# Block-sparse attention fused with a gated FFN: PSUM as eight banks that are taken singly or in pairs, with a new order of all work

## The chip, the cores and the metric

The kernel runs on one core of one Trainium2 chip. The time is that of the device, in microseconds (us): the median over several executions of the same program. Beside it there is one profiled execution, taken by the hardware profiler, whose records give the start and end of every instruction on each engine. The engines are PE (TensorE, matrix multiplications; PEld is its loading of weights), ACT (ScalarE), DVE (VectorE), POOL (GpSimd) and SP (SyncE); POOL and SP do nothing here but issue transfers. An "L352" is line 352 of the kernel.

## The reference: what is computed

Attention for 4 batches, 8 heads, 768 positions and a head dimension of 64, with a mask of 32 x 32 blocks, and behind it an FFN on the 3072 tokens, 512 to 1536 to 512, with a sigmoid gate. Cut to what matters:

```python
scores = scale * np.matmul(q, k.transpose(0, 1, 3, 2))          # scale = 1/8
mask = np.abs(blk_i - blk_j) <= 1                               # blocks of 32
mask = mask | (blk_i == 0) | (blk_j == 0) | (blk_i == n_blocks - 1) | (blk_j == n_blocks - 1)
...                                                             # and 3 sampled key blocks a query block
scores = np.where(mask, scores, -1000000000.0)
attn = softmax(scores)                                          # written out in the reference
x = np.matmul(attn, v)                                          # heads side by side: [3072, 512]
gate = 1.0 / (1.0 + np.exp(-(x @ w_gate)))
out = gate * (x @ w_val) @ w_out
```

## The kernel before: units, tiles and an order written out by hand

**Units.** The work is cut into 12 units: 4 batches times 3 blocks of 256 queries (`UQ`). A unit has four head pairs (`Pair`, L599), a pair has three steps of 256 keys (`Step`, L554). One step is one *score job*: eight matmuls of 64 rows (`qk`, L562) write the scores of two heads into two banks of PSUM, an exp on ACT (L586, 1024 columns) brings them as P to SBUF, and a product with the mask on DVE (L592) clears what is masked. Unit 0 has no product: there, eight more matmuls (from `bias` and `mb`, the mask as rows, and `e`, a constant that spreads them) add the mask to the scores ahead of the exp.

When the three steps of a pair are through, P times V follows (PV). In units 0 and 1 (`WIDE_PV`) it has 24 matmuls of 128 rows (`pv`, L611), a reciprocal (L655) and a product (L656), together called the norm, and four transposes on PE with a copy (`turn`, `evac`), which give xT, the FFN's input. In later units PV is done in 64-row halves (`pv_parts`, L626), a reduction on DVE folds the two halves (L646), and the turn is a transposing DMA on SP's queue (`xbar`, L705).

**FFN.** It goes by groups of units (`GROUPS`: units 0 to 3 alone, then in twos). `Ffn.f` (L774) multiplies xT by the weights of gate and value (wg, wv), ACT makes a tanh of half the gate half (L801; the sigmoid is written as tanh), DVE makes (tanh + 1) times the value half (L804). `y` (L858) multiplies by wo; ACT or DVE copies the rows out with a factor 0.5 (L886, L888) and SP stores them (L878). The very last rows go through `y_last` (L944). Unit 0's FFN (`WIDE`) is in matmuls of 128 rows, all others' in 64-row halves that take turns on two banks (`turns`, L354). In unit 0 the first two jobs (`EARLY`) are cut in two: the first three quarters need three of the four head pairs.

**PSUM.** Four tiles of two banks (128 x 2 x 512 float32), `units_ps[0]` to `[3]`, named m0 to m3 (m in the profile). Each job takes a whole pair of banks, a small one too: a mask tile (two matmuls of 256 columns and a copy, `mask_tiles`, L436), a transposition of q or k (`halves`, L460; `prep`, L478), a 128-row PV, a turn. Nearly all matmuls are issued in one line (`tiled`, L352).

**Loads.** All of q, k, v and the weights come through POOL's DMA queue (L226, L236, L241). Batch 0 and the weights come in a fixed sequence (`FIRST`); for batches 1 to 3 each of 36 loads of two heads is a task of its own, which waits for the last copy that reads the old contents, and for a score job that the order names. For batch 0, q and k are transposed on PE; from batch 1 on, DVE pairs the heads up (L525) and SP's queue transposes (L536). DVE copies v beside a column of ones (`vcopy`, L545).

**The order.** `Plan` (L122) holds some 1200 tasks. `ORDER` is a list of tokens that says in which order they are issued, hence the sequence on every engine and queue:

```python
i, eng, slot, gate = re.fullmatch(r"(\d+)([PADGS]?)(?::(\d))?(?:@(\d+))?", token).groups()
```

`34:1` is task 34 with its result in PSUM pair 1; `8D` is task 8 on DVE (`A`: ACT); `105@30` is load 105, which waits for score job 30; `j3` issues idle matmuls into pair 3 (`idle`, L325), which keep PE running while it has nothing else. The costs that stand at each `plan.add` are for the program that found the order; they don't enter the kernel.

Of the kernel before, what the change touches and what calls it, by code (L numbers as in the profile page):

```python
# [16 lines left out]
ALU = mybir.AluOpType  # L17
# [14 lines left out]
PE, ACT, DVE, DMA, SP = "PADGS"  # L32
# [4 lines left out]
EARLY = 2  # L37
# [3 lines left out]
j3 j3 j3 j3 j3 j3 j3 j3 5A 8D j3 0 11A j3s 9:0 j3s j3s j3s 10D j3s j3s 12:1 1:2 j3s 13A 3:0 2 j3s 34:1 4D 35 15:2  # L41
j3s 32:3 16D 6:0 33 17:1 7D 117:2 18D 97:0 118D 44:1 98A j3s 22:3 78:2 23D 45 36:0 79D 20:3 37 21D
40:2 25:1 30:3 41 26D 76:0 77D 46:1 31 54:2 19 74:0 47 75D 27:3 24 55 50:0 28D 80:1 64:3 51 81D
48:2 65 60:1 49 56:0 61 14 66:3 58:2 67D 105@30 57 29 89:3 59 38:1 90 52:0 86:2 53D 87 39 68:3
93:0 69D 62:1 108:2 94 42:3 109 43D 102:0 63D 111:3 70:1 103 110 126:2 71D 112 104 95:0 84:1 96D
122:3 85A 113 140:0 127 123 91 130:1 128 132:3 141 129 131 72:2 119:0 99:1 73D 133 120 147:2 134
100 135 142 157:0 148 154:3 171:1 124 155 149 158 88 164:3 143:2 156 176:0 92@164 144 121 146@111
101 172 170@44 165 173 161:2 217@54 145 190:1 177 189@46 162 125@40 178 237@54 159 186:3 191 150:2
115:0 151D 192 174:2 187 116 204:1 175 188 231:0 179:3 183:2 232 205 180D 244:3 184 233 206 166
245 82:0 200:2 218 83D 201 246 234:3 193:0 219 194A 152 235 185 153 211:2 136:0 220 137D 212 138  # L50
272:3 195 139 229 223A 202 167:0 255:2 168 236 273 213 221A 239 214:0 230 307:1 274 169 215 275
256 240 216 197:3 308 257 196 181 198 258 248:0 309 182 199 241:2 249 242 310 268:3 262 225:1 250
260 114@268 263 269 251 252:2 226 318:0 261 207:3 319 253 315:1 208 289:2 316 160@315 254 106:0
265:3 243 290 107A 247@265 266 270 276:1 209 291 300:0 293:3 277 301 278 282:1 294 292 283 297 163
303:0 335:2 295 302 222 304 279 227 285:1 336 296 286 238 359:0 305 337 360 210 284 331:3 228
362:1 348 332 361 264 349 363 333 328:0 287 350 329 267 322:3 351A 320 344:1 353A 311:0 323
203@344 345 341:2 387:3 321@359 312 342 317 271@282 426:1 373:0 313 411@300 427 330 397:2 374 398
343 388 346 375 259 408:1 376 389 355:2 400@268 409 390 347@30 419:0 356 334@89 380:3 405:1 428
370:2 381 306@111 364 420 288@44 406 371 386@214 366:3 421 410 365@265 454:2 422 433:1 455 432@380
# [3 lines left out]
442 474:1 484:0 463A 378 465A 339 467:2 452 340 475 524:3 480 485 525 514 354 515:1 327 468 486  # L63
# [4 lines left out]
538 583 438 550:1 567 571 542 439 586 551 638:0 563:2 572 425 539 564 552 595:1 573A 404 577:2 604  # L68
639 574 596 578 609:0 568 597 555 575A 627:2 598 616:3 610 628 617 543@616 635:1 565 712@200 630:2
611 569@300 636 612 592:3 446@563 688:0 631 593 658@60 689 654 706:1 556@231 588:3 707 579 641@550  # L70
640 642:0 632 676@471 619:1 633 589 587@282 620 594 691@214 623:2 690 613 590 670:1 591 643 671
637 605:3 624 644 621 606 645 659:1 618 625 709:0 681:3 710 626 660 607 655:2 682 692:0 656 453
663:3 711 726@99 661 657 608@234 673:2 693 662 674 622@652 664 672 694 548 699:1 695 665 723:2 666
# [3 lines left out]
762 669 782 730:3 745A 734:0 760 757:2 731 735 753 798:3 703 758 799 732 736 764:0 759 750 743A  # L77
600 765 797 826:3 823:1 767 763 824 650 816:0 766 651 827 809:1 756 768 810 719 800 787:3 817 769
733 788 806:1 801:0 807 770D 819:3 789 772A 811 737:1 790:2 839 738 614 802 580 615 791 803 601
# [5 lines left out]
904 856 925 936:0 978:1 913 937 911 857 919:3 979 908 875:0 920 914 876 929:1 921 917A 905 932  # L85
970:3 930 935 971 877 922 946:0 915A 1024:3 931 947 893 1025 928 1027:2 1012:0 939 938 916 1013
948 959:3 1028 966 1040:0 940 960 1041 1026 941 967:2 973:3 944A 942D 968 945 1029 952:0 1001:1
# [6 lines left out]
1078 1074 1094 1008 1082 1095 1083 1084 1100:1 1087A 1096A 1108:3 1088 1098A 1101 1085A 1099 1097  # L94
# [3 lines left out]
1163:2 1154D 1164 1159 1156D 1155 1157 1165 1160 1166 1167 1168:0 1161 1169 1170 1162 1171 1172  # L98
"""
GAP, PV_HALF, PV_PARTS, F_HALF, Y_ONE = 0.3, 0.36, 0.74, 0.875, 0.216  # L100
# [14 lines left out]
class Bank:  # L115


    def __init__(self):
        self.slot = None


class Plan:  # L122
# [14 lines left out]
    def run(self):  # L137
        done = set()
        for token in self.order:
            if token[0] == "j":  # L140
                self.idle(int(token[1]), token[2:])
                continue
            i, eng, slot, gate = re.fullmatch(r"(\d+)([PADGS]?)(?::(\d))?(?:@(\d+))?", token).groups()
            i = int(i)
            engines, fn, deps, more = self.tasks[i]
            assert i not in done and done.issuperset(deps)
            done.add(i)
            if slot is not None:
                more["take"].slot = int(slot)
# [7 lines left out]
def kernel(  # L157
# [159 lines left out]
    units_ps = [ps.tile([128, 2, 512], f32, name=f"m{i}") for i in range(4)]  # L317

    def both(bank):
        return units_ps[bank.slot]  # L320

    def both16(bank):
        return units_ps[bank.slot].bitcast(f16)

    def idle(unit, kind):  # L325
        n = 1 if kind == "s" else 4
        for i in range(2):
            rows = slice(i * D, (i + 1) * D)
            nc.tensor.matmul(
                units_ps[unit][:, i, 0 : n * 128].rearrange("a (x n) -> a x n", n=128),  # L330
# [61 lines left out]
    rings["pr"] = [qp[:, p] for p in range(NP)]  # L392
# [42 lines left out]

    def mask_tiles(c0, c1, j):  # L436

        bank = Bank()

        def mm(eng):  # L440
            for i in range(2):
# [716 lines left out]
```

## Time and profile before

| | before |
|---|---|
| median of 3 runs | 277.87 us (277.65, 277.87, 278.82) |
| the profiled execution: span | 277.8 us |
| its last instruction ends (end of the chain of waits) | 277.84 us |
| granted TensorE clock in it | 0.999 |
| first matmul that isn't idle work | 4.64 us |
| first FFN matmul | 23.94 us |
| last matmul ends | 274.69 us |
| instructions on PE, DVE, ACT, POOL | 5007, 421, 243, 69 |
| moved by DMA | 28.93 MB |

How to read it: the span runs from the first to the last record of the profiled execution; its difference to the median (0.03 us) is smaller than the spread of the runs. "Busy" is the share of the span in which an engine had an instruction at work; as matmuls are pipelined and their ends are modelled, a busy PE is not PE at its peak, and the pace of PE is better read from one matmul's start to the next one's. A matmul of 256 columns starts every 0.11 us; two 64-row matmuls that lie in different halves of the array run beside each other and share this time. In the page's second part the span is cut into 40 slices of 6.9 us with the busy tenths of each: PE has 8, 8, 7, 9 in the first four, then 9 throughout and 5 in the last.

### The profile page before, as it was taken

What the parts mean: (1) busy time and instruction counts of PE and PEld (TensorE: products, weight loads), DVE (VectorE), ACT (ScalarE), POOL (GpSimd) and SP (SyncE); (2) the same over time, 40 slices, a digit from 0 to 9 for tenths busy, and PEclk for the clock granted to TensorE, in tenths of its full rate; (3) what the DMA queues carried; (4) which work ended last, traced back from release to release, by engine and by line L of the source; (5) the groups of instructions that cost most, each with busy time, mean ns of one, the idle gap of its engine ahead of it and who ended that gap; (6) DMA issues with size and microseconds to landing.
All of it is one profiled execution on the core that took longest, in us unless ns stands there. A gap on an engine that the chain in (4) does not pass through costs nothing.

```text
span 277.8 us, 11169 instructions
## 1 busy us (share of the span) xinstructions
PE 270.0 (97%) x5007; PEld 178.7 (64%) x5007; DVE 207.1 (75%) x421; ACT 192.1 (69%) x243; POOL 47.3 (17%) x69
## 2 busy tenths in 40 slices
PE   8879999999999999999999999999999999999995
PEld 3667785896897798655566655655655676555543
DVE  4667788899999989978988886887876899004422
ACT  3988868899989958968868965679688571035300
POOL 7776261030480000028300000000000000000000
PEclk9999999999999999999999999999999999999999
DMA  7999999994599693339986743014130002230004
GB/s 160 175 195 197 200 205 198 140 139 100 84 160 145 117 140 97 103 98 167 142 113 113 73 61 97 2 21 142 24 96 4 4 2 76 70 151 2 0 2 151
DMA packets 56684, 28.93 MB, mean 104 GB/s; under 512 B 33036, under 2 KB 53692, under 8 KB 56636
## 3 DMA queue, kind: packets, MB, share of 16 engines
q0 software_dynamic: 21520, 13.90, 35.7%
q1 hardware_dynamic: 34628, 14.02, 24.8%
q8 instruction: 39, 0.64, 1.0%
q10 hardware_dynamic: 488, 0.30, 0.3%
q14 instruction: 9, 0.07, 0.1%
HBM read 28.47 MB, written 6.29 MB: 125 GB/s over the span
## 4 chain that ended last, share of the span: by engine, by line
PE 87%; DMA 7%; POOL 2%; ACT 1%; DVE 1%; issue 1%; SPq 0%
PE m L352 86%; DMA q<-in_q_dram 3%; DMA v<-in_v_dram 2%; DMA kT<-kp 1%; ACT P L586 1%; POOL k L226 1%; POOL q L226 1%; POOL wg L236 0%; POOL wv L236 0%; DVE ysb L888 0%; DVE P L592 0%; ACT ysb L886 0%; PE m L472 0%; PE m L467 0%; ACT ysb L929 0%
## 5 line engine op out<-in xcount | busy, mean ns | idle before, releaser
L586 ACT ACTIVATE P<-m 128x1024 f16<-128x1024 f32 x144 | 143.1, 1025 | 27.8 <-PE m L352 24.6
L352 PE MATMUL m<-xT,wg 64*128 64x512 f16 (+2 forms) x720 | 136.7, 326 | 0.1
L352 PE MATMUL m<-xT,wv 64*128 64x512 f16 (+2 forms) x720 | 136.7, 326 | 0.0
L592 DVE TENSOR_TENSOR P<-P,mask 128x1024 f16<-128x1024 f16 x132 | 87.0, 684 | 2.7 <-ACT P L586 2.6
L352 PEld LDWEIGHTS <-wg 64*128 64x128 f16 (+1 forms) x720 | 66.6, 94 | 21.2 <-issue 0.8
L352 PEld LDWEIGHTS <-wv 64*128 64x128 f16 (+1 forms) x720 | 66.4, 94 | 18.2 <-issue 0.5
L804 DVE SCALAR_TENSOR_TENSOR ht<-th,m 128x512 f16<-128x512 f32 x72 | 49.0, 685 | 37.0 <-ACT th L801 36.1
L352 PE MATMUL m<-wo,ht 64*128 64x512 f16 (+2 forms) x564 | 70.4, 372 | 0.0
L801 ACT ACTIVATE th<-m 128x512 f32<-128x512 f32 x72 | 42.8, 598 | 29.6 <-PE m L352 26.1
L352 PE MATMUL m<-qT,kT 64*128 64x256 f16 x576 | 53.6, 269 | 0.9 <-DMA kT<-kp 0.5
L352 PEld LDWEIGHTS <-P 64*128 64x128 f16 (+1 forms) x2112 | 41.1, 94 | 5.2 <-issue 0.4
L352 PEld LDWEIGHTS <-ht 64*128 64x128 f16 (+1 forms) x564 | 29.4, 94 | 23.4 <-issue 1.3
L352 PE MATMUL m<-vex,P 64*128 64x65 f16 (+1 forms) x2112 | 42.5, 190 | 0.0
L352 PEld LDWEIGHTS <-kT 64*128 64x128 f16 x576 | 26.7, 94 | 17.8 <-issue 1.3
L646 DVE TENSOR_REDUCE acc<-m 128x260 f32<-128x520 f32 x40 | 27.8, 697 | 7.9 <-PE m L352 6.8
L226 POOL DMA_DIRECT2D k<-in_k_dram x15 | 11.1, 744 | 48.3 <-PE m L352 45.0
L886 ACT ACTIVATE ysb<-m 128x512 f32<-128x512 f32 x18 | 10.2, 601 | 11.8 <-PE m L352 11.8
L656 DVE TENSOR_TENSOR x<-acc,rz 128x256 f16<-128x256 f32 x40 | 17.0, 425 | 1.4
L226 POOL DMA_DIRECT2D v<-in_v_dram x16 | 11.6, 736 | 33.5 <-PE m L352 12.9
L226 POOL DMA_DIRECT2D q<-in_q_dram x19 | 13.9, 733 | 3.9 <-DMA wo<-in_moe_w_out_dram 1.8
L352 PE MATMUL m<-bias,e 64*128 64x256 f16 x48 | 5.9, 271 | 2.3 <-DVE mask L299 1.9
L929 ACT ACTIVATE ysb<-m 128x256 f32<-128x256 f32 x1 | 0.4, 383 | 10.1 <-PE m L352 10.1
(47 smaller groups left out, 84.1 us busy)
## 6 DMA issues: line engine op xcount, KB each, us to landing
out_dram<-ysb SPq DMA_DIRECT2D x23, 256.0 KB, 2.4
v<-in_v_dram POOLq DMA_DIRECT2D x16, 192.0 KB, 5.1
k<-in_k_dram POOLq DMA_DIRECT2D x15, 192.0 KB, 6.6
q<-in_q_dram POOLq DMA_DIRECT2D x12, 192.0 KB, 6.4
wg<-in_moe_w_gate_dram POOLq DMA_DIRECT2D x6, 256.0 KB, 8.4
wv<-in_moe_w_val_dram POOLq DMA_DIRECT2D x6, 256.0 KB, 9.0
wo<-in_moe_w_out_dram POOLq DMA_DIRECT2D x3, 512.0 KB, 12.8
xT<-x SPq DMA_TRANSPOSE x40, 2.4
```

What stands on the lines that cost most here:

```text
L226: return nc.gpsimd.dma_start(dst[:, h0:h1, t0:t1, :], src[b, h0:h1].rearrange("h (p t) d -> p h t d", t=NT)[:, :, t0:t1, :],)
L352: return nc.tensor.matmul(out, lhsT, rhs, start=start, stop=stop, skip_group_check=True).ins
L586: nc.scalar.activation(self.pt.rearrange("a h i n -> a (h i n)"), both(self.bank).rearrange("a h n -> a (h n)"), AF.Exp, bias=0.0, scale=SCALE
L592: nc.vector.tensor_tensor(self.pt, self.pt, m.unsqueeze(1).broadcast_to([128, 2, 2, UQ]), op=ALU.mult,)
L646: nc.vector.tensor_reduce(self.acc.rearrange("a h s d -> a (h s d)"), self.parts.rearrange("a r n -> a n r"), axis=mybir.AxisListType.X, o ...
L656: nc.vector.tensor_tensor(self.x16.rearrange("a s h d -> a h s d"), self.acc[:, :, :, 0:D], rz.broadcast_to([128, 2, 2, D]), op=ALU.mult,)
L801: nc.scalar.activation(th, both(bank)[:, 0, :], AF.Tanh, bias=0.0, scale=0.5)
L804: nc.vector.scalar_tensor_tensor(self.ht[:, tiles[0] : tiles[-1] + 1, :], in0=th.rearrange("a (f n) -> a f n", n=self.w), scalar=1.0, in1= ...
L886: nc.scalar.activation(ysb, both(bank)[:, s, :], AF.Copy, bias=0.0, scale=0.5)
L929: nc.scalar.activation(ysb, src, AF.Copy, bias=0.0, scale=0.5)
```

## The change

**PSUM.** One tile of eight banks, `m` [128, 8, 512]. `units_ps[0]` to `[3]` are now views of two banks each, and `one(bank)`, `one16(bank)` give a single bank, named by the letters a to h (a and b are the halves of pair 0). A slot in `ORDER` may be a digit (a pair) or a letter (one bank), and the letter Q is a new "engine" that picks a task's single-bank form for the planner.

```diff
-    units_ps = [ps.tile([128, 2, 512], f32, name=f"m{i}") for i in range(4)]
+    banks = ps.tile([128, 8, 512], f32, name="m")
+    units_ps = [banks[:, 2 * i : 2 * i + 2, :] for i in range(4)]
...
+    def one(bank):
+        i = "abcdefgh".index(bank.slot)
+        return units_ps[i // 2][:, i % 2, :]
```

**Small work in one bank.** The two mask rows up to 512 columns, the mask tiles, the transpositions of q, k and x (`halves` becomes `turned_in` and `turned_out`) and the PV of units 0 and 1 may take one bank. A mask tile in one bank has both its matmuls in rows 0 to 63, one after the other, where in two banks they lie in different rows; a transposition in one bank is one of 128 x 128 in place of two or four of 64 rows.

```diff
-                    both(bank)[:, i, 0 : c1 - c0],
-                    e64[i * D : (i + 1) * D, t * 128 : (t + 1) * 128],
-                    mb24[i * D : (i + 1) * D, c0:c1],
-                    True,
-                    True,
+                    half(i), e64[rows, t * 128 : (t + 1) * 128], mb24[rows, c0:c1], True, True
...
+        def half(i):
+            return one(bank)[:, i * w : (i + 1) * w] if bank.single else both(bank)[:, i, 0:w]
...
+                rows = slice(0, D) if bank.single else slice(i * D, (i + 1) * D)
```

**FFN of units 0 and 1 in pieces.** For groups below `SMALL = 2`, `Ffn.f` gives way to `f1`, which makes one feature tile: eight matmuls of 128 rows and 256 columns into one bank, a tanh of 256 columns and a product of 256 columns, where `f` makes two feature tiles in two banks with 512 columns each. So unit 1, which was in 64-row halves, is now in 128 rows as well. `EARLY` goes from 2 jobs to 4 pieces. The ring of tanh results is halved for them (`th1`).

```diff
-EARLY = 2
+EARLY, SMALL = 4, 2
...
+        def f1(self, f):
...
+                def mm(eng):
+                    for c in cs:
+                        for g in range(2):
+                            bank.last = tiled(
+                                one(bank)[:, g * UQ : (g + 1) * UQ],
+                                (wg, wv)[g][:, c, f * 128 : (f + 1) * 128],
+                                self.x[:, c, :],
+                                c == 0 and g == 0,
+                                c == 3 and g == 1,
+                            )
...
+            def tanh(eng):
+                nc.scalar.activation(th, one(bank)[:, 0:UQ], AF.Tanh, bias=0.0, scale=0.5)
...
+            if self.g == 0 and f < EARLY:
+                a = plan.add(
+                    [(PE, 0.659)],
+                    go(range(3)),
...
+                a = plan.add([(PE, 0.22)], go(range(3, 4)), [a] + xdone[0][3:], mode="W")
```

**The last rows.** `y_last` writes to one bank instead of the first of two.

**The planner's view.** All costs at `plan.add` are new, and tasks carry what they need of the first transfers (`needs`), their mode on PE and the queue of their transfer; transfers of loads, stores and transposes are planned as one queue (`dma="L"`, `"O"`, `"T"`, `"X"`). None of it enters the kernel but by the order.

**The order.** `ORDER` is all new. The first lines of it, before and after:

```diff
-j3 j3 j3 j3 j3 j3 j3 j3 5A 8D j3 0 11A j3s 9:0 j3s j3s j3s 10D j3s j3s 12:1 1:2 j3s 13A 3:0 2 j3s 34:1 4D 35 15:2
-j3s 32:3 16D 6:0 33 17:1 7D 117:2 18D 97:0 118D 44:1 98A j3s 22:3 78:2 23D 45 36:0 79D 20:3 37 21D
+8 11A 5 j2 j2 j2 j2 j2 j2 j2 j2 j2 6Q:a 9:1 12:2 0 1:b 3:3 13 2 10 7A 30:0 15:1 4A 31 16 34:3 35
+17Q:e 18 117Q:f 118 97Q:c 98 44:0 45 82Q:d 83 20:2 21 32:3 33 80Q:c 81 36:0 37 22Q:d 23 74Q:e
```

What the two programs hold, counted from their instructions: 5007 matmuls before and 4861 after (128-row ones take the place of 64-row pairs, idle ones go from 19 tokens to 9); 235 activations on ACT before and 245 after; 79 and 93 gate and bias products on DVE; copies on ACT 7 and 5, on DVE 67 and 69. POOL's 65 and SP's 64 transposing and 27 copying transfers are the same, and each of the 36 later loads has its gate in both. The first FFN matmul is the 438th matmul before and the 378th after. From it to the end, PE changes 15 times between 128-row and 64-row work before, and 32 times after.

More of the change, by code (lines that the diff above doesn't have):

```diff
@@ L31 @@
 NU = S // UQ
-PE, ACT, DVE, DMA, SP = "PADGS"
+PE, ACT, DVE, DMA, SP, ONE = "PADGSQ"
 VB = 5
@@ L46 @@
[L46 to L57, printed above, removed]
@@ L429 @@
         ),
-        [(DVE, 0.42)],
+        [(DVE, 0.335)],
     )
     t_rows = [
-        rows(S, lambda eng, spread: copy(eng, mb24, spread), [(DVE, 0.95), (ACT, 0.82)])
+        rows(S, lambda eng, spread: copy(eng, mb24, spread), [(DVE, 0.87), (ACT, 0.70)])
     ]
@@ L498, in turn @@
                 tiles = [pr[:, t, :] for t in range(t0, t1)]
-            halves(both16(bank), tiles)
+            turned_in(bank, tiles)
         def evac(eng):
@@ L664, in turn @@
             x16 = self.x16.rearrange("a s h d -> a s (h d)")
-            halves(both16(self.bank2), [x16[:, s, :] for s in range(2)])
+            turned_in(self.bank2, [x16[:, s, :] for s in range(2)])
         def evac(self, eng):
@@ L692, in value @@
                 a, free = plan.add(
[L693 removed]
+                    [(DVE, 0.609)], self.fold, [a] + folded[-3:-2], free=self.bank
                 ), None
             self.normed = plan.add(
[L696 removed]
+                [(DVE, 0.55)], self.norm, [a] + before("x16", self.i), free=free
             )
@@ L748, in scores @@
             take=run[0][1].bank,
-            ops=16 if first else 8,
+            score=True,
+            needs=("e0", "e1") if first else (),
         )
@@ L753, in scores @@
             e = plan.add(
-                [(ACT, 0.98)], st.exp, [a] + before("P", 3 * pr.i + st.j), free=st.bank
+                [(ACT, 0.903)], st.exp, [a] + before("P", 3 * pr.i + st.j), free=st.bank
             )
@@ L844, in f @@
                     take=bank,
-                    lag=GAP,
-                    ops=16 * self.per,
+                    needs=wneeds,
                 )
                 a = plan.add(
-                    [(PE, F_HALF)], half(False), [a], ops=16 * self.per
+                    [(PE, 0.863 if self.w == 512 else 0.872)], half(False), [a], turn=True
                 )
             used["xT"][self.g].append(a)
-            c = plan.add([(ACT, 0.57)], tanh, [a] + before("th", i), free=bank, part=1)
-            g = plan.add([(DVE, 0.68)], gate, [c], free=bank, part=1)
+            old = before("th", i)
+            if i < len(rings["th"]) and used["th1"]:
+                old = [x for m in (2 * i, 2 * i + 1) for x in used["th1"][max(k for k in used["th1"] if k % 6 == m)]]
+            c = plan.add([(ACT, 0.477)], tanh, [a] + old, free=bank)
+            g = plan.add([(DVE, 0.598)], gate, [c], free=bank)
             used["th"][i] = [g]
@@ L898, in part @@
                     take=bank if first and f0 == 0 else None,
-                    lag=0.0 if f0 < 8 else GAP if first else None,
-                    ops=16,
+                    turn=not first and f0 == 0,
+                    needs=(f"o{f0 // 4}",),
                 )
```

296 lines of the change are left out of this document (176 added, 120 removed), and 50 rows, old and new, of the table ORDER.

## The prediction

> **What bounds the kernel now.** I read the page's busy line first, then the chain of waits, then busy time in five stretches.
>
> ```profile
> span 277.8 us, 11169 instructions
> ...
> PE 270.0 (97%) x5007; PEld 178.7 (64%) x5007; DVE 207.1 (75%) x421; ACT 192.1 (69%) x243; POOL 47.3 (17%) x69
> ```
> ```profile
> 206.30 68.39 PE m L352 x884
> ...
> 274.71 0.38 ACT ysb L929
> ```
> ```profile
> 0.00:24.00 24.00, 19.99 (x438) 13.71 (x439) 14.70 (x41) 17.80 (x21) 17.75 (x28) 1.00 1.21 180
> 24.00:60.00 36.00, 35.94 (x668) 28.50 (x666) 29.74 (x62) 29.72 (x39) 10.85 (x16) 1.00 1.24 179
> 60.00:160.00 100.00, 99.47 (x2172) 70.33 (x2170) 90.23 (x186) 84.57 (x104) 18.66 (x26) 1.00 0.76 119
> 160.00:240.00 80.00, 79.88 (x1447) 47.96 (x1441) 61.98 (x120) 50.48 (x65) 0.00 (x0) 1.00 0.20 51
> 240.00:277.80 37.80, 34.67 (x307) 18.21 (x302) 10.47 (x16) 9.50 (x17) 0.00 (x0) 0.99 0.16 58
> ```
>
> The columns are the stretch, its length, then the busy time of PE, PEld, DVE, ACT and POOL, the granted clock, the DMA share and GB/s. From 24 us on PE is busy 250.0 of 253.8 us, and 3.1 us of the rest lie behind its last matmul (274.69). So the kernel has two parts: a start of 24 us in which PE waits for others, and 250 us in which its own stream is the bound. A gain must come from the start, from the few holes later, or from a shorter stream. The start in rows of the timeline (start, duration, engine, line, what; in brackets the idle time and what ended it):
>
> ```profile
> 5.67 0.27 PE L413 MATMUL m<-e,mb 64*128 64x256 f16 x1
> ...
> 15.36 0.29 PE L352 MATMUL m<-bias,e 64*128 64x256 f16 x2 [1.91 <-DVE mask L299]
> 15.47 0.29 PE L352 MATMUL m<-qT,kT 64*128 64x256 f16 x2
> ...
> 19.70 0.91 PE L352 MATMUL m<-vex,P 128*128 128x65 f16 x24
> 20.54 0.23 PE L467 MATMUL m<-const,x 64*128 64x64 f16 x4
> ...
> 22.85 0.61 PE L352 MATMUL m<-qT,kT 64*128 64x256 f16 x8 [0.29 <-DVE x L656]
> 23.69 0.32 PE L472 MATMUL m<-const,q 64*64 64x64 f16 x16 [0.23 <-DMA q<-in_q_dram]
> 23.94 0.28 PE L352 MATMUL m<-xT,wg 128*128 128x256 f16 x1
> ```
> ```profile
> 6.73 1.94 ACT L586 ACTIVATE P<-m 128x1024 f16<-128x1024 f32 x2 [0.86 <-PE m L352]
> 8.56 0.59 ACT L297 CAST mask<-m 128x512 f16<-128x512 f32 x1
> 9.17 5.69 ACT L586 ACTIVATE P<-m 128x1024 f16<-128x1024 f32 x6
> 16.01 4.82 ACT L586 ACTIVATE P<-m 128x1024 f16<-128x1024 f32 x5 [1.15 <-PE m L352]
> ```
> ```profile
> 14.35 0.36 DVE L545 COPY vex<-v 128x768 f16<-128x768 f16 x1 [1.53 <-DMA v<-in_v_dram]
> 14.63 0.68 DVE L299 CAST mask<-m 128x512 f16<-128x512 f32 x1
> ...
> 17.49 0.18 DVE L655 RECIPROCAL rz<-m 128x4 f32<-128x4 f32 x1 [0.60 <-PE m L352]
> 17.70 0.42 DVE L656 TENSOR_TENSOR x<-m,rz 128x256 f16<-128x256 f32 x1
> ```
>
> PE's real supply opens with the first FFN matmul (23.94): it needs unit 0's outputs, so all twelve exps of unit 0, which ACT makes one after another. In them lie a mask copy (0.59) and a hole of 1.15 us: PE stood 1.91 us for a PSUM pair that DVE had not emptied, because a v copy at the head of DVE's queue waited 1.53 us for its load and a mask copy stood behind it.
>
> **The change part by part.** The sum is made on the profiled execution: span 277.84, the same as its chain's end; the median of the runs is 277.87, so 0.03 is added at the end.
>
> *One tile of eight banks.* The names change, no instruction. In the built program each wait of PE for ACT or DVE still goes with a bank or operand that both touch, so I count nothing.
>
> *The start.* First exp: it needs the bias row and ACT free. ACT now also copies the 768-column mask row before it; ACT's 383 and 601 ns for 256 and 512 columns (rows below) extrapolate to 0.82. Its second matmul ends at 5.94 (5.67 above), so it ends near 6.75, and the first exp stays at 6.7 to 6.8. Then twelve exps: two took 1.94 and six 5.69, so each further one 0.94 and one alone 1.0. The mask copies are all on DVE now and go through single banks, so the next scores have pairs of their own. The v copies are ordered behind the masks, not in front. By the order, scores 11 and 12 stand behind two PVs, each with a norm of 0.6; I allow 0.5 for that. Its end: 6.7 + 11 x 0.94 + 1.0 + 0.5 = 18.5. Now the twelfth is the fourth of the five at 16.01: 16.01 + 3 x 0.94 + 1.0 = 19.8. After it stand: the turn and copy of pair 1 (0.2 + 0.3) behind which DVE's norm of pair 2 waits (0.6), PE's PV of pair 3 and two scores beside it, then turn, copy, and FFN: 0.2 + 0.3 + 0.2, with semaphores and a mode change 0.6 more: 2.7 us. FFN opens at 21.2. In the kernel before that stretch takes 4.1 us, with the q transposes ahead of FFN waiting for their load (0.23); they now come after three FFN pieces. Bounds for this term: 20.6 (no wait of scores 11 and 12) to 22.5 (DVE one mask copy and one norm later).
>
> The work that PE has left then: in the order of instructions 437 matmuls stand ahead of the first FFN matmul before, 377 after. Left over additionally are one score job and one q turn (0.22 + 0.11); three mask tiles and one turn are done (0.33 + 0.05). Net -0.05. The mask tiles cost PE twice as much in one bank (their halves run one after the other, 9 x 0.11 = 1.0), but all nine lie before FFN, where PE has room.
>
> *Does FFN find its weights?*
>
> ```profile
> 20.66 0.75 POOL L236 DMA_DIRECT2D wv<-in_moe_w_val_dram  x1
> ```
> ```profile
> wv<-in_moe_w_val_dram POOLq DMA_DIRECT2D x6, 256.0 KB, 9.0
> ```
>
> The fourth pair of weight blocks (feature tiles 6 and 7) is issued last at 20.66 and lands 9.0 later, at 29.7. In the new order it is used behind six FFN pieces (eight matmuls 0.11 apart, by 25.05 and 25.16 below, 0.88 each), nine score jobs of 0.22, one PV of 0.73 (19.70 to 20.54, less one change of mode), turns of 0.3 and twelve mode changes of 0.1: 21.2 + 9.5 = 30.7. Margin 1.0, so nothing; the other blocks have as much.
>
> *Mode changes.* The new order alternates 128-row work (FFN of units 0 and 1) with 64-row work (scores, PV parts). Rows of the same timeline at such a place:
>
> ```profile
> 25.05 0.27 PE L352 MATMUL m<-xT,wg 128*128 128x256 f16 x1
> 25.16 0.27 PE L352 MATMUL m<-xT,wv 128*128 128x256 f16 x1
> 25.36 0.23 PE L467 MATMUL m<-const,x 64*128 64x64 f16 x4
> 25.43 0.27 PE L352 MATMUL m<-mb,e 64*128 64x256 f16 x2
> 25.54 0.84 PE L352 MATMUL m<-qT,kT 64*128 64x256 f16 x8
> ```
>
> 0.20 from the last 128-row start to the next, where 0.11 is the pace: a change costs 0.09 to 0.10. From the first FFN matmul to the end the order has 15 such changes before and 32 after: 17 x 0.10 = +1.7. Bounds: 0 (the wait falls in a hole anyway) and 1.7. I take 1.7, since PE has no holes there. The Trainium skill, page "TensorEngine Tiling (Array Packing)", section "Tiling Modes", says the same against the change: changing the tiling mode, not just the tile, drains the engine. It gives no price there; by the 128 cycles at 2.4 GHz that the Trainium skill's page "TensorE: Matmul & The Clock Gate", section "Part 2: What happens when you issue a matmul", gives for a drain, an estimate is 0.053 a change, 0.9 in all, and the sum would be 0.8 lower. The trace agrees that a change stalls, and at 0.09 it measures the higher price.
>
> *Unit 1 in 128 rows, and half-size pieces.* A pair of 64-row matmuls of 256 columns also goes every 0.11 (15.36, 15.47). So the 96 matmuls of unit 1 cost the same to what two decimals tell, 0 to 0.3; taken 0.1. ACT and DVE do 24 tanhs and gates of 256 columns in place of 12 of 512:
>
> ```profile
> L886 ACT ACTIVATE ysb<-m 128x512 f32<-128x512 f32 x18 | 10.2, 601 | 11.8 <-PE m L352 11.8
> ```
> ```profile
> L929 ACT ACTIVATE ysb<-m 128x256 f32<-128x256 f32 x1 | 0.4, 383 | 10.1 <-PE m L352 10.1
> ```
>
> 24 x 0.383 - 12 x 0.601 = +2.0 us of ACT, and by DVE's 0.42 (L656, 256 columns) and 0.68 (L299, 512) 1.9 there, within 20 to 65 us, where each is busy 0.83 of the time (24 to 60): hidden. Without that cover it would cost at most 2.0.
>
> *Holes in the dense part.* Three are to be seen:
>
> ```profile
> 121.35 0.90 PE L352 MATMUL m<-vex,P 64*128 64x65 f16 x48
> 122.78 0.39 PE L352 MATMUL m<-qT,kT 64*128 64x256 f16 x4 [0.53 <-DMA kT<-kp]
> ```
> ```profile
> 205.80 0.38 PE L352 MATMUL m<-qT,kT 64*128 64x256 f16 x4
> 206.30 0.37 PE L352 MATMUL m<-xT,wg 64*128 64x512 f16 x1
> ```
>
> 0.53 for batch 2's transposes; 0.28 at 206 (0.50 passes where four score matmuls at 0.11 a pair need 0.22); 0.23 at 25.54 (eight score matmuls took 0.84, 0.61 at 22.85). Sum 1.0, removed. For the first: in the order the loads of batch 2 stand 12 to 19 us of PE work earlier (one 48), those of batch 3 38 to 57, on the same gpsimd queue, and the two transposes that the late scores read stand 18 and 22 us ahead of their use. New holes of the new order: from below 0; from above one of 0.5 in each of the three stages, 1.5. I take 0.5. The DMAs are the same in number and bytes.
>
> *The end.* y of the last unit in single banks: same matmuls, the last ACT copy (0.38) and store stay: 277.84 - 274.69 = 3.15. Half a MB more of output leaves within the last 8 us, issued before the last three copies, so 0 (to 0.5).
>
> Sum: 21.2 + (274.69 - 23.94 = 250.75) - 0.05 + 1.7 + 0.1 - 1.0 + 0.5 = 273.2 for PE's last matmul; + 3.15 + 0.03 = **276.4**.
>
> **The rivals.** A measurement of this kernel tells about 0.5% (1.4 us) from no change, so "faster" is below 276.5, "slower" above 279.3.
>
> *B, the start keeps its length.* DVE has three more copies of 0.68 in the stage where it already stood behind loads; if a norm or v copy waits behind two of them, FFN opens at 22.5 and the mode changes eat the rest: 277.7. For it: the chain from 16 to 24 us runs over DVE. Against it: DVE was busy only 14.7 of the first 24 us.
>
> *C, slower: pieces wait for their bank.* In unit 1's FFN banks a and b are used four and three times, with about 2.05 us of PE work between a piece's end and the next one in its bank (one piece 0.88, one PV 0.73, two scores 0.22 each). The bank is free after a tanh (0.38) and a gate (0.43); if an exp (1.02) and a mask product (0.68) stand ahead of them, after 2.5. Each of the 24 pieces of units 0 and 1 that finds that waits 0.45; PE runs in order, so all later work waits too. It decides the sign from seven pieces on (3.1 us: 279.5); eight give 280.0. For: ACT and DVE are at 0.83 there. Against: the order puts the tanh before the queued exps at most places, and eight banks serve.
>
> *D, all goes well.* The changes of mode fall where PE would wait for a bank, and no hole comes: 276.4 - 1.7 - 0.5 = 274.2. Against it: the rows show the 0.09 between streams that waited for nothing.
>
> That nothing is gained because the banks still depend on each other as one tile is the case that the change does not do what it says; it would serialize PE with ACT at each score job (144 x 1 us), and the built program's waits exclude it; no chance is kept.
>
> **How the numbers follow.** Forecast A 0.55, with its own range 275.4 to 277.3 (0.36 of it under 276.5, 0.19 within the bound); B 0.18 (0.17 the same, 0.01 slower); C 0.13 (slower); D 0.14 (faster). Faster 0.50, same 0.36, slower 0.14. The range leaves out C's 0.12 and the lower half of D, 0.07: 274.6 to 278.8. Its ends are also what the open terms give: start 20.6, no changes' price in part and no holes; start 22.5 with 1.5 us of holes.
>
> **What would show it.** The first FFN matmul at 21.2 +- 0.6; the last exp of unit 0 at 18.5; no idle row of 1 us between 7 and 21 us on ACT; 0.2 from start to start at each change from 128 to 64 rows, 32 of them after; no wait for kT near 122; PE busy all but 1 us from 24 us to its last matmul near 273.2; 3.1 us behind it. Wrong it would be by waits of PE for tanh or gate of units 0 and 1 (C), by a first FFN matmul later than 22 (B), or by a hole in the middle whose releaser is a DMA: a load that a DVE copy waits for with products queued behind it.

## The result, and the profile after

The change makes the kernel slower: 297.52 us (median of 4 runs, 295.99 to 298.0) against 278.35 us (median of 4), a ratio of 1.065 with a 95% interval of 1.060 to 1.070. The forecast was 276.4. Ratios and intervals, here and below, leave out executions in a slow state, so a ratio can differ a little from that of the medians.

The page of the kernel after, in its parts 1, 2 and 4 (PEclk is the granted clock and DMA the busy share of the DMA engines, in tenths, one digit for 7.4 us):

```profile
span 296.1 us, 10891 instructions
...
PE 277.1 (94%) x4861; PEld 187.6 (63%) x4861; DVE 210.2 (71%) x437; ACT 190.3 (64%) x251; POOL 47.2 (16%) x69
...
PEclk9999999799979989999999999999999999999999
DMA  8999998979999996983300201221011101001013
...
PE 78%; DVE 8%; DMA 8%; issue 3%; SPq 1%; ACT 1%; DVEq 0%
```

The same stretches as before (length, busy time of PE, PEld, DVE, ACT, POOL, then the granted clock, the DMA share and GB/s):

```profile
0.00:24.00 24.00, 22.22 (x401) 15.45 (x402) 17.58 (x49) 19.09 (x22) 18.51 (x29) 1.00 1.21 177
24.00:60.00 36.00, 32.17 (x573) 23.49 (x572) 28.32 (x65) 27.30 (x42) 9.47 (x14) 0.95 1.16 176
60.00:160.00 100.00, 89.81 (x1910) 71.69 (x1904) 85.62 (x181) 77.51 (x99) 19.26 (x27) 0.97 0.94 125
160.00:240.00 80.00, 80.00 (x1522) 51.14 (x1520) 62.33 (x120) 52.48 (x66) 0.00 (x0) 1.00 0.14 39
```

The start is better, as forecast. The loss lies between 24 and 160 us alone: PE, which was idle for 0.6 of these 136 us, is now idle for 14.0, and there only the granted clock falls below 1.00. Behind 160 us PE is busy throughout. The DMA share tells where to look: 0.94 instead of 0.76 from 60 to 160 us, and in the slices six nines in a row, from 67 to 111 us.

What ends PE's holes, in the timeline of PE (start, duration, what; in brackets the idle time and what ended it):

```profile
55.34 1.03 PE L366 MATMUL m<-qT,kT 64*128 64x256 f16 x8 [3.83 <-DMA kT<-kp]
56.31 0.40 PE L366 MATMUL m<-xT,wg 128*128 128x256 f16 x1
56.49 0.42 PE L366 MATMUL m<-xT,wv 128*128 128x256 f16 x1
56.71 0.42 PE L366 MATMUL m<-xT,wg 128*128 128x256 f16 x1
...
76.38 0.40 PE L366 MATMUL m<-qT,kT 64*128 64x256 f16 x4 [1.00 <-DMA qT<-qp]
85.14 0.27 PE L366 MATMUL m<-xT,wg 64*128 64x256 f16 x1 [4.28 <-DMA xT<-x]
86.57 0.37 PE L366 MATMUL m<-xT,wg 64*128 64x256 f16 x1 [1.04 <-DMA xT<-x]
...
103.36 0.39 PE L366 MATMUL m<-xT,wg 64*128 64x256 f16 x1 [3.11 <-issue]
```

Each releaser that is named is a transposing transfer from SP's queue: of k, of q or of x (the profile names none for 103.36). After the long holes the matmuls start every 0.21 us in place of 0.11 (56.49, 56.71) for some 3 us. How long the transposes take is in the profile's list of transfers, for those issued between 60 and 104 us (number, KB each, median us from issue to landing). After:

```profile
v<-in_v_dram POOLq DMA_DIRECT2D x8, 192.0 KB, 9.1
k<-in_k_dram POOLq DMA_DIRECT2D x8, 192.0 KB, 11.7
q<-in_q_dram POOLq DMA_DIRECT2D x7, 192.0 KB, 10.3
out_dram<-ysb SPq DMA_DIRECT2D x3, 256.0 KB, 10.7
xT<-x SPq DMA_TRANSPOSE x9, 11.6
qT<-qp SPq DMA_TRANSPOSE x5, 10.9
kT<-kp SPq DMA_TRANSPOSE x4, 9.1
```

Before, in the same stretch:

```profile
v<-in_v_dram POOLq DMA_DIRECT2D x5, 192.0 KB, 4.8
out_dram<-ysb SPq DMA_DIRECT2D x3, 256.0 KB, 2.4
k<-in_k_dram POOLq DMA_DIRECT2D x4, 192.0 KB, 5.8
q<-in_q_dram POOLq DMA_DIRECT2D x4, 192.0 KB, 6.4
xT<-x SPq DMA_TRANSPOSE x10, 3.1
qT<-qp SPq DMA_TRANSPOSE x3, 2.5
kT<-kp SPq DMA_TRANSPOSE x3, 3.3
```

23 loads stand there instead of 13, and a transpose of x takes 11.6 us instead of 3.1. The transposes come on another queue than the loads, and yet these five transfers of the kernel after land in the order of issue (us):

```
             issued   landed   us
k load        65.87    77.45   11.58
xT            65.89    77.62   11.73
q load        66.58    78.35   11.77
xT            67.20    78.65   11.45
k load        67.80    79.64   11.84
```

So my theory, number 1 below: the transfers of all queues stand in one line, and the new order has put the loads of batches 2 and 3 into the stretch in which the transposes of x, q and k are asked for. Two rivals: number 2, SP's own queue, where a transpose stands behind another transfer that waits for DVE; number 3, the change itself (waits for single banks, small pieces, more changes of mode).

The loss, worked out from the starts of the matmuls from the first FFN matmul to the end of the last matmul (250.74 us before, 271.20 after, so +20.46): starts that come over 0.25 us later than the pace, 0.98 before and 15.47 after (+14.5); changes between 128-row and 64-row work, 1.37 and 2.93 (+1.6); smaller delays, nearly all of them the half pace behind holes, 0.36 and 3.78 (+3.4); the rest +1.0.

### The profile page after: what moved, and what is told of

The parts are those of the page before. It is cut to its first block, busy times and chain, and to the rows that moved or that the text cites. A ratio compares the mean times of both kernels' runs of the same rounds, so it can differ in the third digit from the quotient of the medians.

```text
span 296.1 us, 10891 instructions
## 1 busy us (share of the span) xinstructions
PE 277.1 (94%) x4861; PEld 187.6 (63%) x4861; DVE 210.2 (71%) x437; ACT 190.3 (64%) x251; POOL 47.2 (16%) x69
## 4 chain that ended last, share of the span: by engine, by line
PE 78%; DVE 8%; DMA 8%; issue 3%; SPq 1%; ACT 1%; DVEq 0%
PE m L366 77%; DMA xT<-x 4%; DVE P L628 4%; DMA kT<-kp 3%; DMA kp<-in_k_dram 1%; DVE x L692 1%; DVE acc L682 1%; SPq L741 1%; ACT P L622 1%; PE m L502 1%; DVE ht L905 0%; DVE qp L561 0%; DVE rz L691 0%; DVE kp L561 0%; SPq L572 0%
## 5 line engine op out<-in xcount | busy, mean ns | idle before, releaser
L366 PE MATMUL m<-xT,wv 64*128 64x512 f16 (+2 forms) x672 | 139.6, 335 | 0.0
L366 PEld LDWEIGHTS <-wg 64*128 64x128 f16 (+1 forms) x672 | 62.9, 96 | 25.5 <-issue 6.3
L366 PEld LDWEIGHTS <-wv 64*128 64x128 f16 (+1 forms) x672 | 62.9, 96 | 24.9 <-issue 6.1
L905 DVE SCALAR_TENSOR_TENSOR ht<-th,m 128x512 f16<-128x512 f32 x60 | 40.5, 684 | 36.4 <-ACT th L902 36.3
L902 ACT ACTIVATE th<-m 128x512 f32<-128x512 f32 x60 | 35.7, 601 | 46.8 <-PE m L366 44.9
L366 PEld LDWEIGHTS <-ht 64*128 64x128 f16 (+1 forms) x564 | 33.0, 94 | 24.2 <-issue 0.4
L366 PE MATMUL m<-vex,P 64*128 64x65 f16 (+1 forms) x2112 | 44.5, 191 | 0.1
L366 PEld LDWEIGHTS <-kT 64*128 64x128 f16 x576 | 29.6, 95 | 17.6 <-issue 4.7
L231 POOL DMA_DIRECT2D v<-in_v_dram x16 | 11.5, 729 | 25.4 <-issue 9.7
L976 DVE TENSOR_SCALAR ysb<-m 128x512 f32<-128x512 f32 x6 | 4.0, 688 | 12.9 <-DMA out_dram<-ysb 8.9
L231 POOL DMA_DIRECT2D k<-in_k_dram x15 | 10.9, 729 | 11.6 <-PE m L366 6.6
L831 ACT ACTIVATE th<-m 128x256 f32<-128x256 f32 x24 | 8.9, 387 | 3.0 <-PE m L366 2.9
## 6 DMA issues: line engine op xcount, KB each, us to landing
k<-in_k_dram POOLq DMA_DIRECT2D x15, 192.0 KB, 11.6
```

The lines of the kernel that those rows point to most:

```text
L231: return nc.gpsimd.dma_start(dst[:, h0:h1, t0:t1, :], src[b, h0:h1].rearrange("h (p t) d -> p h t d", t=NT)[:, :, t0:t1, :],)
L366: return nc.tensor.matmul(out, lhsT, rhs, start=start, stop=stop, skip_group_check=True).ins
L831: nc.scalar.activation(th, one(bank)[:, 0:UQ], AF.Tanh, bias=0.0, scale=0.5)
L902: nc.scalar.activation(th, both(bank)[:, 0, :], AF.Tanh, bias=0.0, scale=0.5)
L905: nc.vector.scalar_tensor_tensor(self.ht[:, tiles[0] : tiles[-1] + 1, :], in0=th.rearrange("a (f n) -> a f n", n=self.w), scalar=1.0, in1= ...
L976: nc.vector.tensor_scalar(ysb, in0=both(bank)[:, s, :], scalar1=0.5, scalar2=None, op0=ALU.mult)
```

## Experiments

All times below are medians; where a ratio stands, it is to the kernel before in the same batch of runs, with its 95% interval. Where no ratio stands, the kernel was run once or its runs scattered.

**Short loads for batches 2 and 3, in the kernel after.** One position in six is loaded, so the output of batches 2 and 3 is another; no instruction, wait or place in the order changes.

```diff
-                lambda eng: load_heads(dst, src, b, 2 * p, 2 * p + 2),
+                lambda eng: load_heads(dst, src, b, 2 * p, 2 * p + 2, 0, 1 if b >= 2 else NT),
```

> The changed kernel, but the loads of batches 2 and 3 bring one position in six (768 values of 64 become 128; the rest of each tile keeps the values of an earlier batch, so the output of batches 2 and 3 is another). Same instructions, order, gates and waits; only the transfers are short. Theory 1 (transfers stand in one line: a transposing transfer issued behind a backlog of loads lands only after them): the transposes of x issued between 60 and 105 us land 2.3 to 5 us after their issue instead of 12, the holes of PE at 76, 85, 87, 95 and 103 us (1.2 + 4.5 + 1.2 + 0.8 + 3.3 = 10.9 us) and the slow clock behind them (about 2.8 us) go, the hole of 4.0 us at 55 us stays, since batch 1's loads are untouched: 283 to 285 us. Rival 2 (the order on SP's queue: a transpose waits behind another that waits for DVE): nothing of that is changed, so most of the holes stay, 290 us or more.

285.82 us, 11.7 less than with whole loads. Transfers issued from 60 to 104 us, and the one hole over 0.25 us that has a named releaser:

```profile
xT<-x SPq DMA_TRANSPOSE x11, 4.9
kT<-kp SPq DMA_TRANSPOSE x5, 3.3
qT<-qp SPq DMA_TRANSPOSE x5, 5.4
```
```profile
56.57 0.61 PE L359 MATMUL m<-qT,kT 64*128 64x256 f16 x8 [3.72 <-DMA kT<-kp]
```

The holes from 76 us on are gone, with SP's queue in the same order: rival 2, as a wait for DVE, falls for them. The hole at 55 us, ahead of which stand batch 1's whole loads, stays, as expected.

**Batch 1's last loads earlier.** Three tokens of the order, each a load with the score job that it waits for:

```diff
-... 125@217 ... 206@261 ... 237@261 ... 257@261 ...
+... 125@217 257@217 237@217 206@217 ...
```

> The changed kernel with one edit: the last three q and k loads of batch 1, which wait for a score job of unit 2's last pair and are issued at 45.8, 46.5 and 47.2 us, in front of three of the transposes, wait for an earlier score job of unit 2 and stand right behind the other five in POOL's queue (34 to 38 us). Theory 1: they land by 50 us, the transpose that PE waits for at 51.3 to 55.3 us lands by 52, the hole of 4.0 us shrinks below 1 and the slow clock behind it (2 us) goes; the holes from 76 us on stay: 291 to 293 us. Rival 2: the order of SP's queue and of DVE is the same, so the hole stays: 297.

292.73 us (one execution), and the hole there is down from 3.83 to 0.96:

```profile
52.99 0.61 PE L359 MATMUL m<-qT,kT 64*128 64x256 f16 x8 [0.96 <-DMA kT<-kp]
```

That hole came from three loads issued just in front of the transposes; no other token was moved.

**Stores on ACT's queue.**

```diff
-                nc.sync.dma_start(
+                nc.scalar.dma_start(
                     out.rearrange("(b p t) m -> b t p m", b=B, t=NT)[b, 2 * u + s],
```

> The changed kernel with the stores of the output (all but the last rows) issued from ACT's queue instead of SP's, so that no transpose stands behind a store that waits for its copy. Theory 1: the holes of PE stay, 295 to 299 us. Rival 2: a good part of the 10.9 us between 76 and 103 us goes, 290 or less.

300.22 us (one execution), a little over what theory 1 allowed, and no gain. The transposes of x from 60 to 104 us take as long as in the kernel after:

```profile
xT<-x SPq DMA_TRANSPOSE x9, 11.2
```

**Short loads for batch 1 as well.** The same edit, for the three later head pairs of batch 1 too.

> The changed kernel with short loads also for head pairs 1 to 3 of batch 1 (as the run with short loads of batches 2 and 3: one position in six, so the output of batches 1 to 3 is another). Same instructions, order, gates and waits. Theory 1: with hardly a load in the line no hole over 1 us is left behind the first FFN matmul, neither at 55 nor from 76 us on, and what stands is the kernel that the prediction summed up: a start that opens FFN at 21.7 to 23, changes of mode of 0.1, 278 to 281 us. Rival 2 (order on SP's queue) and rival 3 (waits for single banks, slow small pieces): holes or waits of several us stay, 284 or more.

280.25 us, ratio 1.005 (1.003 to 1.008). Page and timeline:

```profile
PE 273.4 (98%) x4861; PEld 187.9 (67%) x4861; DVE 209.2 (75%) x437; ACT 190.1 (68%) x251; POOL 47.4 (17%) x69
```
```profile
54.91 0.61 PE L359 MATMUL m<-qT,kT 64*128 64x256 f16 x8 [1.04 <-DMA kT<-kp]
```

One hole of 1.0 is left behind the first FFN matmul. From there to the end of the last matmul it takes 252.95 us, 2.2 more than before (250.74). Single banks, small pieces and changes of mode are all still there, so rival 3 is worth no more than these 2.2 of the 20.5 us. The prediction's sum for that part is 252.0, with 0.5 for holes that here are 1.2.

**Control: the same short loads in the kernel before.**

> Control: the kernel before with the short loads of batches 2 and 3 (one position in six, so the output of batches 2 and 3 is another). Theory 1: in the kernel before these loads come in two bursts, at 72 to 82 and at 123 to 138 us, in which hardly a transpose is asked for, so making them short gives at most its hole of 0.5 us at 122: 277 to 278.5 us. If short loads gained 3 us or more here too, the gain of 11.7 us that they gave in the changed kernel would not be due to its order.

278.36 us, ratio 0.9998 (0.997 to 1.002): nothing. Short loads gain 11.7 us only where the order has put loads among transposes.

**The kernel before with loads among its transposes.** One effect of the change alone: eight loads of batch 3 stand earlier, nothing else is touched. Two of them:

```diff
-617 543@616 635:1 565 712@200 630:2
+617 635:1 565 630:2
...
-280 384 402 429:2
+280 543@383 384 402 429:2
...
-438 550:1 567 571
+438 712@566 550:1 567 571
```

> The kernel before with one part of the change's effect: the eight q and k loads of batch 3 stand right behind the copies that free their buffers (and wait for the score job just ahead), six of them some 30 us of PE work earlier, amid the transposes of 91 to 105 us, as they do in the changed kernel. Everything else is the kernel before. Theory 1: the loads stand in one line with the transposes, which land 4 to 8 us later where they were 2.3 to 4.4; PE then waits for one of them, so 1 to 8 us are lost (279 to 286 us), with holes of PE that end with a transposing transfer between 95 and 125 us. Rival 2 and rival 3: SP's queue, PSUM and PE's order are those of the kernel before, so nothing changes, 277.5 to 278.5 us.

290.14 us, ratio 1.036 (1.028 to 1.044); the medians are 11.6 us apart, more than the 8 I had allowed. The chain of waits, and PE's timeline:

```profile
119.86 11.22 DMA kT<-kp
```
```profile
131.13 0.61 PE L345 MATMUL m<-qT,kT 64*128 64x256 f16 x4 [5.90 <-DMA kT<-kp]
131.53 0.63 PE L345 MATMUL m<-xT,wv 64*128 64x512 f16 x1
131.54 0.63 PE L345 MATMUL m<-xT,wg 64*128 64x512 f16 x1
131.96 0.63 PE L345 MATMUL m<-xT,wv 64*128 64x512 f16 x1
```

Two more starts came 1.8 and 1.3 us late, at 100 and 106. This kernel has the PSUM, the tiles and PE's order of the kernel before. Its four executions took 286.16 to 290.48.

**The same with six loads.** The last two stand where they stood, the first of them behind the score job of unit 6, and with it all that follows in POOL's queue.

```diff
-635:1 565 712@200 630:2
+635:1 565 712@616 630:2
```

> The kernel before with six of batch 3's q and k loads amid the transposes of 91 to 105 us, as in the run with eight, but the other two and all that follow in POOL's queue wait for the same late score job of unit 6 that opens them in the kernel before. So the kT transpose which took 11.2 us amid five loads at 119.9 us has none in front of it or behind it. Theory 1: it lands 2.5 to 4 us after its issue, the hole of 6.1 us at 125 to 131 us and the slow clock behind it (1.4 us) go, the holes of 1.8 and 1.3 us at 100 and 106 us stay: 281.5 to 284 us. Against theory 1 it would be if the hole at 125 stayed although no load stands near: 289.

282.02 us, ratio 1.013 (1.011 to 1.016). From 107 to 198 us no matmul starts more than 0.25 late: the hole of 5.9 has gone with the five loads (117.8 to 121.9) that stood around that transpose. The late starts at 100 and 106 stay (0.9 and 2.2).

**Five orders with the loads spread out,** in the kernel after: the first by hand, the others by a reckoning with one line for all transfers. In the first four only later loads, with the DVE copies and SP transposes behind them, stand elsewhere, and PE's order is untouched; the fifth moves tasks of all engines. An example from the second, one load of batch 3 (673), its copy (682) and its transpose (683):

```diff
-437:2 438 371 673@437 440:0
+437:2 438 440:0
...
-431 682 423 465:3
+431 423 465:3
...
+377 387:1 388 673@376 478@376
...
+494 543 570 682 683 509
...
-615 517 683 518 519
+615 517 485 518 519
```

> The changed kernel with the loads of batches 2 and 3, and the DVE copies and SP transposes that follow each, moved later in the order: one load per 2.5 us of PE work from 49 us on for batch 2, one per 3 us from 84 on for batch 3, each copy 10 us of PE work behind its load; each load's gate is the score job just ahead of it. All bytes move, in full. Theory 1: no backlog, holes from 76 us on gone, the one at 55 stays: 282 to 286 us. Rival 2 expects some gain as well, since SP's queue is thinned out between 60 and 105 us, but holes of several us where a transpose of batch 2 or 3 still stands in front of one of x: 288 to 294.

> The changed kernel; only the 36 later loads with their gates, the DVE copies and the SP transposes of q and k behind them stand elsewhere in the order: loads of batch 1 earlier (the last q and k load of it is issued 4 us of PE work earlier, most of the others 5 to 20), those of batch 3 spread over 62 to 145 us of PE work where they stood at 56 to 89, its transposes at 87 to 139 where they stood at 87 to 106. PE's, ACT's and the other orders as in the changed kernel, all bytes moved. Theory 1: most of the 15.5 us of holes and of the slow clock goes; two or three holes of 0.5 to 2.5 us where batch 1's transposes are late: 279 to 285 us. Rival 3 (single banks, small pieces, changes of mode make the change slow): none of these is touched, 294 or more.

> The changed kernel with the 36 later loads, their gates, and the copies and transposes of q and k behind them in other places once more: all q and k loads of batch 1 by 32 us of PE work (the last stood at 43), batch 2's transposes at 58 to 82, batch 3's loads over 75 to 125 and its transposes at 94 to 130, each copy into the paired tile behind the transpose that reads the old contents. All orders of PE and ACT as in the changed kernel, all bytes moved. Theory 1: 279.5 to 284 us, holes of 0.8 to 2 us at 44 to 54 us only; not below the 280.3 of the run with short loads by more than its start can vary, since that has no line to wait in. Rival 3 (single banks, small pieces): 294 or more.

> As the run before it with other places for the same tokens (batch 3's loads at 55 to 132 us of PE work, some of batch 1's loads as early as 4 us, ahead of the weights). Theory 1: 279 to 286 us, with one hole of about 3 us near 45 us, where an early load of batch 1 stands in front of the q of unit 1. Rival 3: 294 or more.

> The changed kernel with tasks of all engines behind the first FFN matmul moved by some places each, so that transposes are asked for early and loads spread: no hole over 0.6 us by a reckoning in which all transfers stand in one line. Theory 1: 278 to 282 us; its own doubt is the changes of mode, of which this order has more (0.1 us each). Rival 3: 290 or more.

296.76 us for the first (it scattered: 291.03, then 296.1 to 297.99), 287.87 for the second (ratio 1.031, 1.024 to 1.039; a fourth execution took 566 us and is left out), 287.66 for the third (1.034, 1.028 to 1.040), 294.84 for the fourth (1.060, 1.053 to 1.066), 301.4 for the fifth (1.084). In the last two the copy of one k pair of batch 3 stands ahead of the transpose that should read batch 2's, so that pair of batch 2 is computed with batch 3's k. All five are above what theory 1 gave them, and the fourth and fifth lie where I had put rival 3; against it, for the fourth, stand the chain below and the 2.2 us that rival 3 can be worth in PE's order, which is the same there. The second and third win back half of the loss; the first between next to nothing and 6.5 us. The fifth lost 5 us behind its last matmul alone, where a copy of output rows waited for a store, and its largest named waits of PE are for exps on ACT (2.0 us in all): its order of PE's work is another, so it tells little of the loads. What is left in the others, in the timeline of the second, of the third, and in the chain of the fourth:

```profile
61.55 0.83 PE L359 MATMUL m<-qT,kT 64*128 64x256 f16 x12 [2.44 <-DMA kT<-kp]
```
```profile
61.08 1.46 PE L359 MATMUL m<-qT,kT 64*128 64x256 f16 x12 [3.57 <-DMA qT<-qp]
```
```profile
84.51 12.64 DMA kT<-kp
```

Still transposes behind loads; and in the second a hole of 1.3 us at 45.6, ahead of which DVE stood 1.2 us for a load of q that one of its copies reads. Theory 1 holds in that the loads among the transposes make the holes. It does not hold as one line in the order of issue: in the kernel after, a transpose of q issued at 68.55 us landed at 83.55, behind a load issued at 70.90 that landed at 83.25. The packets, the pieces in which a transfer is moved, tell more. From 76 to 82 us of the kernel after, for the queue of the loads (q0) and that of SP (q1), packets, MB and share:

```profile
q0 software_dynamic: 1138, 0.82, 98.7%
q1 hardware_dynamic: 1145, 0.28, 47.6%
```

In nearly every half microsecond of it each queue has about 100 packets: the two take turns, packet by packet. A load and a transpose of x have 256 packets each, one of q or k has 768. Counted off by packets, the transpose of x issued at 67.20 was on its way for about 1.4 us beside some 270 packets of loads, where one without loads took 0.5 (issued at 105.92 in the kernel before). But its first packet started only some 9 us after its issue, behind the earlier transposes of SP's own queue: those of q and k took 4 to 5 us each beside the loads, and mostly 0.8 to 1.7 in the kernel before without them. So SP's queue has its part after all, not by a wait for DVE as in number 2, but because the loads slow whatever stands in it. With SP's queue empty a transpose behind loads still starts late: 3.7 us after its issue (62.27 in the kernel after), and 1.2 without loads.

My reckoning had none of this. In landings behind the weights, over the kernels with whole loads: two loads that stand next to each other land 1.0 to 1.3 us apart (median, by which pairs one counts), with a transpose of x between them 1.4, with one of q or k 2.2. Transposes of q and k that follow one another land 0.55 to 0.63 apart (55.29, 55.84, 56.47 in the kernel after). So one that stands between two loads takes about twice the time of one among its like. The order before keeps them apart: nearly all its loads of batches 2 and 3 come at 72 to 82 and at 123 to 138 us, and of its 64 transposes one is issued in these stretches.

No version here beats the kernel before. With hardly a load in the line the new order is 0.5% behind it (280.25), so other places for the loads alone would hardly make it faster than that; another order of PE's own work was not tried for its own sake.

## Why the prediction was wrong, point by point

- *The start* was right in this trace: the first FFN matmul was to come at 21.2, and came at 21.68; the last exp of unit 0 was to end at 18.5, and ended at 18.97. In the nine other traces of the new order and its variants it is 21.7 to 24.0, five of them past the 22 that I had named as the sign of rival B; in the latest the first load of POOL's queue landed at 7.48 us instead of 6.77, and the clock was 0.50 from 7.59 to 11.00. So the gain at the start, 2.3 us in this pair of traces, is not a steady one.
- *Changes of mode* were right: 0.2 us from start to start, and 1.7 us in all, measured 1.6. The timeline after, at the first one:

```profile
22.33 0.27 PE L366 MATMUL m<-xT,wg 128*128 128x256 f16 x1
22.44 0.27 PE L366 MATMUL m<-xT,wv 128*128 128x256 f16 x1
22.64 0.61 PE L366 MATMUL m<-qT,kT 64*128 64x256 f16 x8
```

- *Unit 1 in 128 rows and half-size pieces*: no hole over 0.25 us was ended by a tanh or a gate of units 0 and 1, so rival C, the one whose sign was slower, did not come about; the rest of the stream is 1.0 longer, where I had 0.1, and no run splits this further.
- *The end* was right: 3.2 us behind the last matmul.
- *Holes in the dense part* is the step that failed. I removed the 0.53 at 122, rightly, and took 0.5 for new holes, at most 1.5; they are 15.5. I had seen that the loads stand 12 to 57 us of PE work earlier. From that I concluded that they come in good time, and that "the two transposes that the late scores read stand 18 and 22 us ahead of their use". I counted the distance in the order and left the time to land at what it was, the DMAs being "the same in number and bytes". But the same bytes asked for amid the transposes make these land later: a transpose of x 11.6 us after its issue in place of 3.1. The short loads show that this is the cause (285.8 and 280.3), the denser loads in the kernel before that it suffices (290.1), and the control that it is not in the loads as such.
- The profile of before had it: a load of batch 1 issued at 30.2 us, behind the weights, took 13.4 us to land, one with none just ahead of it 3.4 to 3.8, and loads issued together landed mostly 0.9 to 1.1 apart (up to 2.6). At these prices, and those of the transposes between loads above, 23 loads and 18 transposes fill 37 to 44 of the 44 us from 60 to 104 (an estimate); measured, the times to land rose by 4 to 8 us.
- *Not in the sum at all*: the half pace behind a long hole, 3.4 us.
- The DMA side was named as what would make the prediction wrong ("a hole in the middle whose releaser is a DMA"), but had no rival, no price and no chance. The upper end of the range, 278.8, held nothing of it.
- *The base* of the sum, a small second error: the 0.03 between span and median, in the table before as in the sum, sets two unlike things side by side. In every later run that has both, the time is 1.72 to 1.87 us longer than the span of the same execution. So the traced execution of the kernel before, with its span of 277.84, stands for a time near 279.6, and the span that the sum forecast, 276.35, for one near 278.1.

## What to carry to other kernels

An order that asks for the same transfers earlier is not the same for DMA: count, for the stretch where they now stand, what each takes, and add it to the time to land of everything urgent that is issued there, on the loads' queue or on another. Here the loads of batches 2 and 3 cost a hole of 0.5 us where hardly a transpose was asked for, and most of 15.5 us of holes among transposes that PE soon needed. When PE is the bound, a gain of 2 us at the start is soon lost to one such wait, and a long hole costs more than its length.

## What the runs showed of the hardware

- While POOL's and SP's queues both have work they take turns packet by packet (1138 and 1145 packets from 76 to 82 us in the kernel after; packets of 768 bytes in the loads, of 256 in the transposes). The Trainium skill, page "Trainium Kernel Development and Optimization", section "Key Constraints", says that transfers of all issuing engines run on the same 16 DMA engines; the traces agree. The Trainium skill's page "DMA: Bandwidth & Descriptors", section "Queues, rings and completion order", has each engine go round between its queues packet by packet; the equal counts agree. It does not follow that a short transpose gets past a backlog of loads: the two of the five transfers listed with the result landed 11.7 and 11.5 us after their issue, the loads beside them 11.6 to 11.8.
- The clock: in 14 traces no idle time of PE of up to 2.44 us behind the first FFN matmul brought a slower pace by itself, and each of 3.11 us or more did, with 0.21 us a matmul of 256 columns instead of 0.11. In the kernel after this lasted about 3 us (103.36 to 106.3, behind an idle time of 3.11; 1.4 us lost); in others longer, at a granted clock of 0.50 (61.1 to 66.3 us in the third of the five orders, 5.2 us). The Trainium skill, page "TensorE: Matmul & The Clock Gate", section "Part 1: The HAM clock gate (the "warmup" mystery)", gives half the clock after an idle window of about 3.4 us; the traces agree roughly, with the change between 2.44 and 3.11. Idle time alone isn't all of it: the kernel with short loads for batch 1 as well had a clock of 0.50 from 7.59 to 11.00 us, with no idle time of PE over 1 us in its trace before that.
